# Where 1/z is applied in an attention kernel: as a scale by partition for tiles turned by DMA, as a row for tiles turned on TensorE

## The chip, the core and the metric

The kernel runs on one core of one Trainium2 chip. The core has five engines that each work through their own list of instructions in order and wait for one another by semaphores: TensorE (PE: matmuls; PEld is its loading of weights), VectorE (DVE), ScalarE (ACT), GpSimd (POOL) and SyncE (SP), which here issues all DMAs. The metric is the device time of one execution in microseconds (us).

## The reference

Two stages, the second on the output of the first. `q` is (4, 12288, 128), `kv` is (4, 384, 32, 128).

```python
kv_pool = kv.reshape(B, H // 4, 4, W // 4, 4, C).mean(axis=(2, 4))
k = v = kv_pool.reshape(B, -1, C) @ w_sr          # 768 keys a batch
s = (q @ k.transpose(0, 2, 1)) / sqrt(C)
a = exp(s - s.max(-1)); a /= a.sum(-1) + 1e-9
x = a @ v                                         # the input of the second stage
gate = sigmoid(causal_conv5(x, conv_w))           # 5 taps along the sequence
out = (gate * (x @ w_val)) @ w_out
```

## The kernel before

A batch has 24 groups of 512 queries, so there are 96 groups, and a group has four tiles j = 0 to 3 of 128 queries. All instructions are written by hand in the order in which each engine runs them; one loop goes over the 384 tiles, and each pass of it also carries steps of earlier and later groups: in the pass of tile j of group g stand the scores of the next tile, a part of the av product of group g-2 (`avg`), the conv of group g-3 (`xg`), the second matmuls of group g-4 (`mg`) and the store of a pair of groups.

A tile's path: `score` (L250) puts 128 x 768 scores into a pair of PSUM banks (there are three pairs; a pair is free again when the tile's low pass has read it). `row_max` (L256, DVE) gives the negated maximum by row. `expo` (L268, ACT) replaces the scores by exp and gives the sum z by row, through a second instruction that reads ACT's accumulator. What follows needs the probabilities with keys on partitions, as two fp16 parts (high, and what high leaves over) of 2^15 times the exp. `p_hi` (L315, ACT) and `p_lo` (L319, DVE, one tile later) make the parts. For tiles 0 to 2 (`NX = 3`) they are made with queries on partitions (`hl`) and turned by DMA (`dma_start_transpose`, L323: tiles 0 and 1 in one DMA, tile 2 in another). For tile 3 exp goes to SBUF (`pf`), PE turns it in six matmuls (`turn`, L298), and both passes work on the turned tile (`pt`). `av_part` (L332) then multiplies `pt` by the split values, 18 matmuls a group in four parts.

The division by z comes at the end: the four sums of a group are columns of a tile `z`, ACT adds 1e-9 (`norm_eps`, L272), DVE takes one reciprocal of 128 x 4 (L275), PE turns it (L278), DVE copies the four rows out (L285), a DMA writes them to DRAM (`rd`), and another reads them back as one row of 512 on all 128 partitions (`rb`, L291). `g_x` (L349) multiplies av by the row and by a scale by partition. The matmul outputs `m` of `norm_turn`, of the value matmul (`g_val`, L388) and of the output matmul (`g_out`, L398) share one PSUM bank.

The keys and values of the next batch are made during the current one: `setup_steps` is a list of steps of which the loop takes one at tile 3 of each group, from the second group of a batch on. The first 16 load pieces of kv (the first one loads three pieces, each later one the piece two ahead) and hand back a pooling (`pool_kv`, L121, DVE) that runs at tile 0 of the next group; then come two projections with key splits, and the value splits. Small DVE work (`trickle`) is dripped into the loop two pieces a tile. The weights of the second stage arrive as 64-bit floats and are converted by 14 DVE instructions (`load_moe`, L90 to L97), of which eight run between the poolings of the first batch, ahead of the loop, and the rest from the third tile of the second group on.

After the loop a tail finishes the last four groups, with the last group cut into halves.

Of the kernel before, what the change touches and what calls it, by code (L numbers as in the profile page):

```python
# [16 lines left out]
P = 128  # L17
GQ = 512
NT = GQ // P
NX = 3  # L20
# [7 lines left out]
def attn_moe_kernel(ctx, tc, qT, kvT, w_sr, w_moe, outT):  # L28
# [165 lines left out]
    trickle = []  # L194

# [63 lines left out]
    def on_pe(j):  # L259

        return j >= NX

    def expo(g, j):
        if j == 0:
            g.z = zs[g.i % len(zs)]
        if on_pe(j):
            g.pf[j] = pfp.tile([P, NK], F32, name="pf")
        nc.scalar.activation(out=halves(g.pf[j]) if on_pe(j) else g.s[j], in_=g.s[j],  # L268
                             func=AF.Exp, bias=g.nm.pop(j), accum_out=g.z[:, j:j + 1])

    def norm_eps(g):
        nc.scalar.activation(out=g.z[:, :NT], in_=g.z[:, :NT], func=AF.Copy, bias=1e-9)  # L272

    def norm_reciprocal(g):
        nc.vector.reciprocal(out=g.z[:, :NT], in_=g.z[:, :NT])  # L275

    def norm_turn(g, m):
        nc.tensor.transpose(m[:, :P], g.z, ident)  # L278
        g.rm = m[:NT, :P]

    def norm_store(g):

        r = small.tile([NT, P], F32, name="r")
        g.rd = dram.tile([NT, P], F32, name="rd")
        nc.vector.tensor_copy(out=r, in_=g.rm)  # L285
        nc.sync.dma_start(out=g.rd, in_=r)

    def norm_rows(g):
        g.rb = work.tile([C, GQ], F32, name="rb", bufs=3)
        row = g.rd.rearrange("(o j) p -> o (j p)", o=1)  # L290
        nc.sync.dma_start(out=g.rb, in_=row.broadcast_to([C, GQ]))  # L291
# [14 lines left out]
    def part(g, j, a):  # L306

        if on_pe(j):
            return pt_tile(g)[:, j, a * NCH:(a + 1) * NCH].rearrange("p (h k) q -> p h (k q)", h=2)
        if g.hl is None:  # L310
            g.hl = hlp.tile([P, NX, 2, NK], F16, name="hl")
        return halves(g.hl[:, j, a])

    def p_hi(g, j):
        nc.scalar.activation(out=part(g, j, 0), in_=g.s[j], func=AF.Copy, scale=2.0 ** 15)  # L315

    def p_lo(g, j):

        nc.vector.scalar_tensor_tensor(out=part(g, j, 1), in0=g.s.pop(j), scalar=2.0 ** 15,  # L319
                                       in1=part(g, j, 0), op0=ALU.mult, op1=ALU.subtract)  # L320
        if j in (1, 2):
            j0 = 0 if j == 1 else j
# [25 lines left out]
    def g_x(g, av, c0=0, c1=GQ):  # L348
        nc.vector.scalar_tensor_tensor(out=g.x[:, HALO + c0:HALO + c1], in0=av,  # L349
                                       scalar=g.st["down"], in1=g.rb[:, c0:c1],  # L350
                                       op0=ALU.mult, op1=ALU.mult)
# [89 lines left out]
    for i in range(PIECES):  # L441
# [5 lines left out]
        if i >= 8 and convert:  # L447
            convert.pop(0)()
# [21 lines left out]
    for t in range(NT * G):  # L470
# [7 lines left out]
        if t == NT + 2:  # L478
# [16 lines left out]
        if on_pe(j):  # L495
# [70 lines left out]
    avs = [bank()[:, :half] for _ in cuts]
    av_range(n1, avs[0], 0, len(AV_ORDER), 0, NT // 2)
    h = g_h(n2.th, n2.m)
    av_range(n1, avs[1], 0, len(AV_ORDER), NT // 2, NT)
    n3.m = g_val(n3, misc())  # L570
    n2.m = g_out(h, bank())
    ths = []
    n1.th = work.tile([C, GQ], F32, name="th")
    for av, c in zip(avs, cuts):
        g_x(n1, av, *c)
        ths.append(g_tanh(conv_dve(n1, *c), n1.th[:, c[0]:c[1]]))
# [3 lines left out]
    n3.th = g_tanh(n3.gate)  # L580
    h = g_h(n3.th, n3.m)
    ms = [g_val(n1, bank()[:, :half], *c) for c in cuts]
    hs = [g_h(th, m) for th, m in zip(ths, ms)]
    n3.m = g_out(h, misc())
# [33 lines left out]
```

## Time and profile before

| what | value |
|---|---|
| median of 3 runs | 1134.94 us (1133.9 to 1135.04) |
| profiled execution | 1133.22 us |
| its span (first to last instruction) | 1131.4 us |
| mean granted clock of TensorE | 0.983 |
| DVE row max, L256 | 384, mean 949 ns |
| DMA, queue of SP | 214.48 MB, 85.4% of 16 engines' span |
| transposes by DMA, L323 | 192 |
| rows of 1/z, `rb` | 96 of 256 KB |

A profile row reads: line, engine, operation, output <- input by the program's names, shapes, count, then busy time and mean duration of one, and idle time of the engine just before with what ended it. A row of the timeline begins with its start and duration in us instead; a bracket at its end is the idle time before it and the engine, tile and line that ended it.

### The profile page before, as it was taken

The page shows a single profiled execution, that of the slowest core. Times are in us where ns is not written, and L with a number is a line of the kernel's source. Part 1 is how long each engine was busy: PE and PEld are TensorE (multiplying, and loading weights), DVE is VectorE, ACT ScalarE, POOL GpSimd, SP SyncE. Part 2 cuts the span into 40 slices and gives each one's busy share as a digit, 9 for nine tenths or more (in the row PEclk, how much of TensorE's full clock was granted, in tenths as well). Part 3 has the DMA queues.
Part 4 walks back from the last instruction along what each step waited for, and adds up shares of the span by engine and source line. Part 5 has one row for each costly group of instructions (what it writes and reads, how often), then busy time and mean ns, then how long its engine had stood idle before and what let it go on. Part 6 is the DMA issues. An engine that isn't in the chain of part 4 may idle for free.

```text
span 1131.4 us, 16595 instructions
## 1 busy us (share of the span) xinstructions
PE 1063.6 (94%) x5174; PEld 715.6 (63%) x5174; DVE 919.0 (81%) x1290; ACT 910.4 (80%) x1659; POOL 864.4 (76%) x948
## 2 busy tenths in 40 slices
PE   2879999999979999999997999999999999999996
PEld 1656666666756666666764666666666666666663
DVE  6868888888858888888885888888888888888884
ACT  1868888888858888888885888888888888888881
POOL 1168788878858888888885888887888888888872
PEclk9989999999989999999998999999999999999998
DMA  7779999887879999888876999898788888888872
GB/s 271 145 178 200 211 210 232 192 178 191 187 169 198 202 224 214 206 177 191 187 165 170 209 217 226 200 221 183 171 171 197 187 170 202 186 170 199 175 148 93
DMA packets 487095, 215.53 MB, mean 190 GB/s; under 512 B 453088, under 2 KB 453856, under 8 KB 487008
## 3 DMA queue, kind: packets, MB, share of 16 engines
q1 hardware_dynamic: 487008, 214.48, 85.4%
q8 instruction: 41, 0.67, 0.2%
q14 instruction: 46, 0.38, 0.1%
HBM read 75.83 MB, written 25.36 MB: 89 GB/s over the span
## 4 chain that ended last, share of the span: by engine, by line
PE 49%; DVE 25%; ACT 11%; issue 6%; POOL 5%; DMA 3%; SPq 1%; DVEq 0%; ACTq 0%
PE s L250 17%; PE av L332 16%; PE m L388 8%; DVE nm L256 8%; POOL ql L236 5%; ACT s L268 5%; DVE pool L121 4%; DVE pt L319 4%; ACT hl L315 4%; DVE x L349 4%; PE m L398 3%; PE s L298 3%; DMA kvt<-in_kv 3%; ACT qh L232 2%; DVE h L393 2%
## 5 line engine op out<-in xcount | busy, mean ns | idle before, releaser
L368 POOL TENSOR_TENSOR sum<-sum,tap 128x512 f32<-128x512 f32 x282 | 359.6, 1275 | 39.7 <-ACT tap L357 17.8
L332 PE MATMUL av<-pt,vh 128*128 128x512 f16 x1140 | 389.1, 383 | 0.0
L256 DVE TENSOR_REDUCE nm<-s 128x1 f32<-128x768 f32 x384 | 364.4, 949 | 3.7 <-PE s L250 3.7
L268 ACT ACTIVATE s<-s,nm 128x768 f32<-128x768 f32 x288 | 251.9, 875 | 125.5 <-DVE nm L256 124.3
L359 POOL TENSOR_SCALAR tap<-x,wm 128x512 f32<-128x512 f32 x376 | 253.4, 693 | 82.4 <-DVE x L349 80.9
L319 DVE SCALAR_TENSOR_TENSOR hl<-s,hl 128x768 f16<-128x768 f32 x288 | 273.1, 948 | 21.0 <-ACT hl L315 20.3
L250 PE MATMUL s<-kh,qh 128*128 128x384 f32 x768 | 253.3, 411 | 10.8 <-DVE hl L319 8.1
L315 ACT ACTIVATE hl<-s 128x768 f16<-128x768 f32 x288 | 233.3, 810 | 9.1
L332 PEld LDWEIGHTS <-vh 128*128 128x128 f16 x1164 | 114.0, 98 | 175.5 <-issue 85.8
L332 PE MATMUL av<-pt,vl 128*128 128x512 f16 x570 | 217.5, 382 | 0.0
L236 POOL TENSOR_TENSOR ql<-q,qh 128x512 fp32r<-128x512 f32 x96 | 121.8, 1269 | 122.6 <-ACT qh L232 122.6
L250 PE MATMUL s<-kh,ql 128*128 128x384 f32 x768 | 199.1, 341 | 0.0
L250 PE MATMUL s<-kl,qh 128*128 128x384 f32 x768 | 198.9, 340 | 0.0
L250 PEld LDWEIGHTS s<-kh,qh 128*128 128x128 f32 x768 | 132.4, 193 | 51.8 <-DVE hl L319 8.4
L349 DVE SCALAR_TENSOR_TENSOR x<-av,down,rb 128x512 f32<-128x512 f32 x95 | 71.4, 751 | 89.6 <-POOL ql L236 71.5
L250 PEld LDWEIGHTS s<-kl,qh 128*128 128x128 f32 x768 | 141.3, 190 | 0.5 <-DVE kl L147 0.5
L250 PEld LDWEIGHTS s<-kh,ql 128*128 128x128 f32 x768 | 140.9, 190 | 0.0
L388 PE MATMUL m<-x,wm 128*128 128x512 f32 x188 | 103.0, 630 | 25.0 <-DVE r L285 24.9
L368 POOL TENSOR_TENSOR sum<-tap,tap 128x512 f32<-128x512 f32 x94 | 120.4, 1281 | 0.0
L393 DVE SCALAR_TENSOR_TENSOR h<-th,m 128x512 f32<-128x512 f32 x94 | 64.7, 689 | 59.2 <-PE m L388 57.7
L315 ACT ACTIVATE pt<-s 128x768 f16<-128x768 f32 x96 | 77.8, 810 | 37.8 <-PE s L298 37.8
L332 PEld LDWEIGHTS <-vl 128*128 128x128 f16 x582 | 57.6, 99 | 77.9 <-issue 55.2
(68 smaller groups left out, 1068.9 us busy)
## 6 DMA issues: line engine op xcount, KB each, us to landing
kvt<-in_kv SPq DMA_DIRECT2D x64, 384.0 KB
rb<-rd SPq DMA_DIRECT2D x96, 256.0 KB
q<-in_q SPq DMA_DIRECT2D x47, 512.0 KB
out<-o SPq DMA_DIRECT2D x46, 512.0 KB
pt<-hl SPq DMA_TRANSPOSE x192
rd<-r SPq DMA_DIRECT2D x96, 2.0 KB
out<-o SPq DMA_DIRECT2D x3, 256.0 KB
q<-in_q SPq DMA_DIRECT2D x2, 256.0 KB
```

What stands on the lines that cost most here:

```text
L236: nc.gpsimd.tensor_tensor(out=g.ql, in0=g.q, in1=g.qh.bitcast(F32), op=ALU.subtract)
L250: nc.tensor.matmul(s[:, h, :HALF], a[:, sl], k[:, h * HALF:(h + 1) * HALF], start=(i == 0), stop=(i == 2))
L256: nc.vector.tensor_reduce(out=nm, in_=g.s[j], axis=AX.XY, op=ALU.max, negate=True)
L268: nc.scalar.activation(out=halves(g.pf[j]) if on_pe(j) else g.s[j], in_=g.s[j], func=AF.Exp, bias=g.nm.pop(j), accum_out=g.z[:, j:j + 1])
L315: nc.scalar.activation(out=part(g, j, 0), in_=g.s[j], func=AF.Copy, scale=2.0 ** 15)
L319: nc.vector.scalar_tensor_tensor(out=part(g, j, 1), in0=g.s.pop(j), scalar=2.0 ** 15, in1=part(g, j, 0), op0=ALU.mult, op1=ALU.subtract)
L332: nc.tensor.matmul(out, g.st[v][:, k * P:(k + 1) * P], g.pt[:, j0:j1, a * NCH + k], start=(i == 0), stop=(i == len(AV_ORDER) - 1))
L349: nc.vector.scalar_tensor_tensor(out=g.x[:, HALO + c0:HALO + c1], in0=av, scalar=g.st["down"], in1=g.rb[:, c0:c1], op0=ALU.mult, op1=ALU.mult)
L359: eng.tensor_scalar(out=g.tap[k], in0=src, scalar1=w, scalar2=1.0, op0=ALU.mult, op1=ALU.mult)
L368: nc.gpsimd.tensor_tensor(out=s, in0=acc, in1=g.tap[k], op=ALU.add)
L388: nc.tensor.matmul(m, wval, g.x[:, HALO + c0:HALO + c1], start=True, stop=True)
L393: nc.vector.scalar_tensor_tensor(out=h, in0=th, scalar=1.0, in1=m, op0=ALU.add, op1=ALU.mult)
```

## The change

Every even group of a batch now has all four tiles turned by DMA (`by_dma = 4`), every odd one three as before. For a tile turned by DMA, z stays a column of its own (`zr`): DVE adds 1e-9 and multiplies by 2^-15 in one instruction and takes the reciprocal in a second one, and both passes of that tile use the result as their scale by partition, in place of the constant 2^15. Only the tile turned on PE keeps the way by row, now with one row of 128 instead of four, and only in odd groups. `norm_eps` is gone from ACT. `g_x` becomes a product with the scale by partition alone for the columns of DMA-turned tiles, and keeps the row for the last 128 columns of odd groups.

In the loop, ACT's other work of a tile (tanh, a tap, the cast of q, the evacuation of an output) now stands between exp and the high pass. On DVE the order of a tile is row max, low pass of the tile before, h (tile 1), reciprocal of this tile. Pooling runs at tile 3, two groups after the step that loaded its first pieces (a batch's list has one step more). The conversions all run in the loop, from its fourth tile on. The transposes of an even group go in two pairs. The tail is written in another order.

```diff
-    def on_pe(j):
-        return j >= NX
+    def on_pe(g, j):
+        return j >= g.by_dma
     def expo(g, j):
-        if j == 0:
-            g.z = zs[g.i % len(zs)]
-        if on_pe(j):
+        if on_pe(g, j):
             g.pf[j] = pfp.tile([P, NK], F32, name="pf")
-        nc.scalar.activation(out=halves(g.pf[j]) if on_pe(j) else g.s[j], in_=g.s[j],
-                             func=AF.Exp, bias=g.nm.pop(j), accum_out=g.z[:, j:j + 1])
-    def norm_eps(g):
...
-    def norm_reciprocal(g):
...
+            g.z = zs[g.i // 2 % len(zs)]
+            g.r[j] = g.z[:, :1]
+        else:
+            g.r[j] = small.tile([P, 1], F32, name="zr")
+        nc.scalar.activation(out=halves(g.pf[j]) if on_pe(g, j) else g.s[j], in_=g.s[j],
+                             func=AF.Exp, bias=g.nm.pop(j), accum_out=g.r[j])
+    def reciprocal(g, j):
+        r = g.r[j]
+        nc.vector.tensor_scalar(out=r, in0=r, scalar1=1e-9,
+                                scalar2=1.0 if on_pe(g, j) else 2.0 ** -15,
+                                op0=ALU.add, op1=ALU.mult)
+        nc.vector.reciprocal(out=r, in_=r)
...
+    def p_scale(g, j):
+        return 2.0 ** 15 if on_pe(g, j) else g.r[j]
     def p_hi(g, j):
-        nc.scalar.activation(out=part(g, j, 0), in_=g.s[j], func=AF.Copy, scale=2.0 ** 15)
+        nc.scalar.activation(out=part(g, j, 0), in_=g.s[j], func=AF.Copy, scale=p_scale(g, j))
     def p_lo(g, j):
-        nc.vector.scalar_tensor_tensor(out=part(g, j, 1), in0=g.s.pop(j), scalar=2.0 ** 15,
+        nc.vector.scalar_tensor_tensor(out=part(g, j, 1), in0=g.s.pop(j), scalar=p_scale(g, j),
                                        in1=part(g, j, 0), op0=ALU.mult, op1=ALU.subtract)
-        if j in (1, 2):
-            j0 = 0 if j == 1 else j
+        if (j % 2 or j == g.by_dma - 1) and not on_pe(g, j):
+            j0 = j // 2 * 2
...
     def g_x(g, av, c0=0, c1=GQ):
-        nc.vector.scalar_tensor_tensor(out=g.x[:, HALO + c0:HALO + c1], in0=av,
-                                       scalar=g.st["down"], in1=g.rb[:, c0:c1],
-                                       op0=ALU.mult, op1=ALU.mult)
+        mid = min(c1, g.by_dma * P)
+        if c0 < mid:
+            nc.vector.tensor_scalar_mul(out=g.x[:, HALO + c0:HALO + mid], in0=av[:, :mid - c0],
+                                        scalar1=g.st["down"])
+        if mid < c1:
+            nc.vector.scalar_tensor_tensor(out=g.x[:, HALO + mid:HALO + c1], in0=av[:, mid - c0:],
+                                           scalar=g.st["down"], in1=g.rb[:, mid - c1:],
+                                           op0=ALU.mult, op1=ALU.mult)
...
     def setup_steps(b, st):
         def piece(i):
             if i == 0:
                 key_tiles(st)
+            else:
+                pooling.append(lambda: pool_kv(st, i - 1))
             for k in range(3) if i == 0 else (i + 2,):
                 if k < PIECES:
                     load_kv(b, st, k)
-            return None, lambda: pool_kv(st, i)
-        steps = [lambda i=i: piece(i) for i in range(PIECES)]
+        steps = [lambda i=i: piece(i) for i in range(PIECES + 1)]
...
+            g.by_dma = 4 - i % 2
...
         row_max(cur, j)
         expo(cur, j)
-        if on_pe(j):
+        if on_pe(cur, j):
             turn(cur, j)
-            norm_eps(cur)
-            if mg:
-                out_tile(mg)
-                g_evac(mg, mg.m)
-        p_hi(cur, j)
         if mg and j == 0:
             mg.th = g_tanh(mg.gate)
         if xg and j == 1:
             tap(xg, TAPS - 1, nc.scalar)
-        if last and j == 0:
-            norm_reciprocal(last)
-        if last and j == 1:
+        if at(gi + 2) and j == 2:
+            g_qh(at(gi + 2))
+        if mg and j == 3:
+            out_tile(mg)
+            g_evac(mg, mg.m)
+        turned = last and on_pe(last, NT - 1)
+        if turned and j == 1:
             norm_store(last)
         drip()
         if prev:
             p_lo(prev, (j - 1) % NT)
+        if mg and j == 1:
+            mg.h = g_h(mg.th, mg.m)
+        reciprocal(cur, j)
+        p_hi(cur, j)
         if low and (j == 0 or t < NT):
             low()
             low = None
-        if last and j == 0:
+        if pooling and j == NT - 1:
+            pooling.pop(0)()
+        if turned and j == 0:
             norm_turn(last, misc())
         drip()
-        if mg and j == 1:
-            mg.h = g_h(mg.th, mg.m)
```

In the tail, after the loop, the av product of the second-last group now comes first, the last low pass and the way of its row of 1/z follow, and the two halves of the last group take turns with the output steps of the two groups before it:

```diff
-    norm_reciprocal(n1)
-    p_lo(n1, NT - 1)
-    store_pair(n5)
+    av_part(n2, 0)
     norm_turn(n1, misc())
     n4.th = g_tanh(n4.gate)
-    norm_store(n1)
-    n4.m = g_val(n4, misc())
-    av_part(n2, 0)
-    norm_rows(n1)
     tap(n3, TAPS - 1, nc.scalar)
     g_conv(n3)
-    h = g_h(n4.th, n4.m)
+    p_lo(n1, NT - 1)
+    norm_store(n1)
+    store_pair(n5)
...
```

More of the change, by code (lines that the diff above doesn't have):

```diff
@@ L19 @@
 NT = GQ // P
-NX = 3
 class Group:
@@ L194, in attn_moe_kernel @@
     trickle = []
+    pooling = []
     def value_steps(st):
@@ L257, in row_max @@
         g.nm[j] = nm
-    def on_pe(j):
-        return j >= NX
+    def on_pe(g, j):
+        return j >= g.by_dma
     def expo(g, j):
-        if j == 0:
-            g.z = zs[g.i % len(zs)]
-        if on_pe(j):
+        if on_pe(g, j):
             g.pf[j] = pfp.tile([P, NK], F32, name="pf")
-        nc.scalar.activation(out=halves(g.pf[j]) if on_pe(j) else g.s[j], in_=g.s[j],
-                             func=AF.Exp, bias=g.nm.pop(j), accum_out=g.z[:, j:j + 1])
-    def norm_eps(g):
-        nc.scalar.activation(out=g.z[:, :NT], in_=g.z[:, :NT], func=AF.Copy, bias=1e-9)
-    def norm_reciprocal(g):
-        nc.vector.reciprocal(out=g.z[:, :NT], in_=g.z[:, :NT])
+            g.z = zs[g.i // 2 % len(zs)]
[10 more added lines that the diff above has]
+        nc.vector.reciprocal(out=r, in_=r)
     def norm_turn(g, m):
         nc.tensor.transpose(m[:, :P], g.z, ident)
-        g.rm = m[:NT, :P]
+        g.rm = m[:1, :P]
     def norm_store(g):
-        r = small.tile([NT, P], F32, name="r")
-        g.rd = dram.tile([NT, P], F32, name="rd")
+        r = small.tile([1, P], F32, name="r")
+        g.rd = dram.tile([1, P], F32, name="rd")
         nc.vector.tensor_copy(out=r, in_=g.rm)
@@ L288, in norm_rows @@
     def norm_rows(g):
-        g.rb = work.tile([C, GQ], F32, name="rb", bufs=3)
-        row = g.rd.rearrange("(o j) p -> o (j p)", o=1)
-        nc.sync.dma_start(out=g.rb, in_=row.broadcast_to([C, GQ]))
+        g.rb = work.tile([C, P], F32, name="rb", bufs=3)
+        nc.sync.dma_start(out=g.rb, in_=g.rd.broadcast_to([C, P]))
     def turn(g, j):
@@ L306, in part @@
     def part(g, j, a):
[L308 removed]
+        if on_pe(g, j):
             return pt_tile(g)[:, j, a * NCH:(a + 1) * NCH].rearrange("p (h k) q -> p h (k q)", h=2)
         if g.hl is None:
[L311 removed]
+            g.hl = hlp.tile([P, NT, 2, NK], F16, name="hl")
         return halves(g.hl[:, j, a])
+    def p_scale(g, j):
+        return 2.0 ** 15 if on_pe(g, j) else g.r[j]
     def p_hi(g, j):
[L315 removed]
+        nc.scalar.activation(out=part(g, j, 0), in_=g.s[j], func=AF.Copy, scale=p_scale(g, j))
     def p_lo(g, j):
[L319 removed]
+        nc.vector.scalar_tensor_tensor(out=part(g, j, 1), in0=g.s.pop(j), scalar=p_scale(g, j),
                                        in1=part(g, j, 0), op0=ALU.mult, op1=ALU.subtract)
[L321 to L322 removed]
+        if (j % 2 or j == g.by_dma - 1) and not on_pe(g, j):
+            j0 = j // 2 * 2
             nc.sync.dma_start_transpose(
@@ L525, in attn_moe_kernel @@
             g_conv(xg)
-        if last and j == 3:
+        if turned and j == 3:
             norm_rows(last)
         if at(gi + 2) and j == 2:
-            g_qh(at(gi + 2))
             g_ql(at(gi + 2))
@@ L563, in attn_moe_kernel @@
     store(n4)
+    avs = [bank()[:, :half] for _ in cuts]
+    for i, av in enumerate(avs):
+        av_range(n1, av, 0, len(AV_ORDER), i * NT // 2, (i + 1) * NT // 2)
     n2.th = g_tanh(conv_dve(n2))
     new_x(n1, n2, nc.scalar.copy)
[L566 to L569, printed above, removed]
-    n3.m = g_val(n3, misc())
[L571 to L576, printed above, removed]
+    g_x(n1, avs[0], *cuts[0])
+    h2 = g_h(n2.th, n2.m)
+    n2.m = g_out(h2, bank())
+    n1.th = work.tile([C, GQ], F32, name="th")
+    ths = [g_tanh(conv_dve(n1, *cuts[0]), n1.th[:, :half])]
+    n3.m = g_val(n3, misc())
+    n3.th = g_tanh(n3.gate)
     out_tile(n2)
@@ L579, in attn_moe_kernel @@
     store(n2)
[L580 to L584, printed above, removed]
+    g_x(n1, avs[1], *cuts[1])
+    h3 = g_h(n3.th, n3.m)
+    ms = [g_val(n1, bank()[:, :half], *cuts[0])]
+    n3.m = g_out(h3, misc())
+    ths.append(g_tanh(conv_dve(n1, *cuts[1]), n1.th[:, half:]))
     g_evac(n3, n3.m)
     store(n3)
-    for h, c in zip(hs, cuts):
-        g_evac(n1, g_out(h, bank()[:, :half]), *c)
+    ms.append(g_val(n1, bank()[:, :half], *cuts[1]))
+    for th, m, c in zip(ths, ms, cuts):
+        g_evac(n1, g_out(g_h(th, m), bank()[:, :half]), *c)
         store(n1, *c)
```

12 lines of the change are left out of this document (6 added, 6 removed).

## The prediction

> **What bounds the kernel now.** I read the page first, then stretches of equal work, then one group engine by engine. "Group" is 512 queries (four tiles of 128); there are 96.
>
> ```profile
> span 1131.4 us, 16595 instructions
> PE 1063.6 (94%) x5174; PEld 715.6 (63%) x5174; DVE 919.0 (81%) x1290; ACT 910.4 (80%) x1659; POOL 864.4 (76%) x948
> ```
>
> TensorE (PE) leads, but an average says nothing of a stage. The next view takes stretches from one row max (L256) to another; its columns are length, busy time and count of L256 alone, granted clock, DMA share and GB/s. Four row maxima make a group.
>
> ```profile
> 28.06:56.97 28.91, 11.38 (x13) 0.94 0.75 144
> 56.97:74.23 17.26, 3.79 (x4) 0.80 0.71 167
> 318.23:338.33 20.10, 3.81 (x5) 0.83 0.82 197
> 592.96:614.09 21.13, 3.80 (x4) 0.76 0.79 193
> 338.33:504.63 166.30, 56.93 (x61) 1.00 0.93 204
> 504.63:538.48 33.85, 11.38 (x12) 1.00 0.93 185
> 858.11:1081.19 223.08, 79.71 (x84) 1.00 0.84 182
> ```
>
> There are four kinds of group. Plain ones take 223.08 / 21 = 10.62 us. Those that also pool a piece of the next batch's kv take 166.30 / 15 = 11.09 (a count of 61 holds the row max at the far edge). Those that project or split keys and values take 33.85 / 3 = 11.28. And three, one for each later batch, take 17 to 21 us. From 56.97 to the last group's start (1091.8) I count 45 pooling groups, the three long ones, 15 with projections or splits, and 29 plain: 1034.8 us. The same stretches with all engines (PE busy first):
>
> ```profile
> 338.33:504.63 166.30, 163.26 (x796) 108.58 (x795) 143.38 (x197) 141.58 (x256) 137.44 (x150) 1.00 0.93 204
> 858.11:1081.19 223.08, 223.08 (x1115) 153.19 (x1114) 183.24 (x253) 195.88 (x358) 192.57 (x210) 1.00 0.84 182
> ```
>
> Plain groups are PE without a gap. Pooling groups lose 0.2 us of PE each, and something more in restarts. The waits name the cause of the long groups:
>
> ```profile
> DVE pool L121 <- DMA kvt<-in_kv: 25.2, 8, 7.0
> 601.86 0.95 DVE L121 TENSOR_REDUCE pool<-kvt 128x48 f32<-128x768 f32 x1 [7.03 <-DMA kvt<-in_kv]
> ```
>
> VectorE (DVE) reaches the first pooling just after its load was issued and stands 7 us; everything behind it stands too, and the clock of that stretch falls to 0.76. Against 11.09 the three cost 6.2 + 9.0 + 10.0 = 25.2 us.
>
> One pooling group, first DVE, then ScalarE (ACT), then PE:
>
> ```profile
> 404.87 0.95 DVE L256 TENSOR_REDUCE nm<-s 128x1 f32<-128x768 f32 x1
> ...
> 406.66 0.94 DVE L121 TENSOR_REDUCE pool<-kvt 128x48 f32<-128x768 f32 x1
> 407.52 0.95 DVE L256 TENSOR_REDUCE nm<-s 128x1 f32<-128x768 f32 x1
> 408.39 0.27 DVE L285 COPY r<-m 4x128 f32<-4x128 f32 x1
> ...
> 409.95 0.69 DVE L393 SCALAR_TENSOR_TENSOR h<-th,m 128x512 f32<-128x512 f32 x1 [0.42 <-PE m L388]
> ...
> 415.29 0.75 DVE L349 SCALAR_TENSOR_TENSOR x<-av,down,rb 128x512 f32<-128x512 f32 x1 [0.86 <-POOL ql L236]
> 415.95 0.95 DVE L256 TENSOR_REDUCE nm<-s 128x1 f32<-128x768 f32 x1
> ```
> ```profile
> 405.86 0.88 ACT L268 ACTIVATE s<-s,nm 128x768 f32<-128x768 f32 x1 [0.25 <-DVE nm L256]
> 406.65 0.19 ACT L268 ACTIVATION_READ_ACCUMULATOR s<-s,nm 128x1 f32 x1
> 406.88 0.81 ACT L315 ACTIVATE hl<-s 128x768 f16<-128x768 f32 x1
> 407.58 0.62 ACT L384 ACTIVATE th<-sum 128x512 f32<-128x512 f32 x1
> ...
> 413.33 0.61 ACT L232 CAST qh<-q 128x512 fp32r<-128x512 f32 x1
> 413.84 0.90 ACT L268 ACTIVATE pf<-s,nm 128x768 f32<-128x768 f32 x1
> ```
> ```profile
> 408.71 1.12 PE L388 MATMUL m<-x,wm 128*128 128x512 f32 x2 [0.20 <-DVE r L285]
> ...
> 412.44 0.38 PE L332 MATMUL av<-pt,vh 128*128 128x512 f16 x1
> ...
> 413.71 0.39 PE L332 MATMUL av<-pt,vh 128*128 128x512 f16 x1
> ...
> 415.02 0.82 PE L298 MATMUL s<-ident,pf 128*128 128x128 f32 x6
> ```
>
> Back to back, a DVE instruction starts 0.085 before the printed end of the one ahead (415.29 + 0.75 against 415.95), an ACT one 0.1 before. A hand-off between DVE and ACT takes about 0.04 (row max ends 405.82, exp starts 405.86). An av matmul is 0.218 apart (six from 413.71 to 415.02), so the scores of a tile take 413.71 - 412.44 - 0.22 = 1.05. ACT now goes straight from exp to the high pass (L315); nothing of DVE stands between them.
>
> **The change, part by part.** Prices of the new instructions come from these rows:
>
> ```profile
> L268 ACT ACTIVATE pf<-s,nm 128x768 f32<-128x768 f32 x96 | 86.8, 905 | 0.0
> L319 DVE SCALAR_TENSOR_TENSOR hl<-s,hl 128x768 f16<-128x768 f32 x288 | 273.1, 948 | 21.0 <-ACT hl L315 20.3 <-DVE r L285 0.4
> L393 DVE SCALAR_TENSOR_TENSOR h<-th,m 128x512 f32<-128x512 f32 x94 | 64.7, 689 | 59.2 <-PE m L388 57.7 <-ACT th L384 1.5
> L275 DVE RECIPROCAL z<-z 128x4 f32<-128x4 f32 x96 | 16.1, 168 | 0.0
> L167 DVE TENSOR_SCALAR pw<-pw 128x1 f32<-128x1 f32 x4 | 0.5, 134 | 0.0
> L374 DVE TENSOR_SCALAR fast<-x,wm 128x512 f32<-128x512 f32 x1 | 0.5, 489 | 0.1
> ```
>
> *PE.* Every second group loses six turning matmuls and the turn of z, 0.6 + 0.1 us, which leaves PE 10.62 - 0.35 = 10.27 a group on average. That is a gain only if nothing else is later.
>
> *Scale by partition.* The high pass now reads a scale per partition. Below: no extra, 0.81 (its row above). Above: exp to SBUF, which has a bias per partition, 0.905. I take 0.905. For the low pass, L349 (a per-partition scalar, 0.75) and L393 (none, 0.69) differ by 0.06: 0.95 to 1.01, I take 1.01.
>
> *Reciprocal per tile.* Two small dependent instructions, 0.14 (L167) and about 0.16 (one column of L275's four), in place of one per group. Their issue is small; their place is not. DVE (the row max of the next tile ends each piece):
>
> ```order
> L256 TENSOR_REDUCE nm<-s 128x1
> L285 COPY r<-m 4x128
> L319 SCALAR_TENSOR_TENSOR hl<-s,hl 128x768
> L393 SCALAR_TENSOR_TENSOR h<-th,m 128x512
> L256 TENSOR_REDUCE nm<-s 128x1
> ```
>
> That is tile 1 before. In the changed kernel, an even group:
>
> ```order
> L257 TENSOR_REDUCE nm<-s 128x1
> L290 COPY r<-m 1x128
> L326 SCALAR_TENSOR_TENSOR hl<-s,zr,hl 128x768
> L405 SCALAR_TENSOR_TENSOR h<-th,m 128x512
> L277 TENSOR_SCALAR zr<-zr 128x1
> L280 RECIPROCAL zr<-zr 128x1
> L257 TENSOR_REDUCE nm<-s 128x1
> ```
>
> The reciprocal stands behind the previous tile's low pass (L326) and h (L405), and ACT's high pass waits for it. So there is now a ring: high pass of tile t, low pass of t, reciprocal of t+1, high pass of t+1. The end of tile 3, in the changed kernel (before, the pooling stood in tile 0, behind L319 pt):
>
> ```order
> L326 SCALAR_TENSOR_TENSOR hl<-s,zr,hl 128x768
> L277 TENSOR_SCALAR zr<-zr 128x1
> L280 RECIPROCAL zr<-zr 128x1
> L120 TENSOR_REDUCE pool<-kvt 128x48
> L358 TENSOR_SCALAR x<-av,down 128x512
> L257 TENSOR_REDUCE nm<-s 128x1
> ```
>
> Pooling and x now come between the last reciprocal and the next group's first row max. Tile 1 on ACT, changed kernel: the filler (tap) has moved between exp and high pass.
>
> ```order
> L271 ACTIVATE s,zr<-s,nm 128x2x384
> L369 ACTIVATE tap_1428<-x,wm 128x512
> L322 ACTIVATE hl<-s,zr 128x768
> L271 ACTIVATE s,zr<-s,nm 128x2x384
> ```
>
> *The ring of an even pooling group*, from its first row max at 0. Row max ends 0.95; exp 0.99; sum read 1.78 to 1.97; scale-and-add 2.01, reciprocal 2.19, row max of tile 1 at 2.27, copy 3.14 to 3.41, which frees the bank for the value matmul at 3.45. From there to h took 1.24 (408.71 to 409.95): 4.69. H issues in 0.605: 5.30; reciprocal 5.48 to 5.64; high pass of tile 1 at 5.68; row max of tile 2 from 5.56 to 6.51, so exp 6.55, read 7.34, qh 7.57, high pass of tile 2 at 8.08 (its reciprocal is ready), ending 8.98; exp of tile 3 at 8.88. Low pass of tile 2 at 9.02, its successor 0.925 later, 9.95; reciprocal 10.13; pooling 10.21; x 11.07; next row max **11.73**. An odd group has no copy: th follows the sum read, high pass of tile 0 at 2.54 to 3.45, low pass 3.49, h 4.42 instead of 4.69, so 0.30 less with rounding; its x is two instructions (384 columns 0.62 and 128 columns 0.35, from L349's rate of 0.53 per 512 plus 0.22), 0.14 more. **11.57**; mean 11.65, against 11.09 now.
>
> *Without pooling*, x waits for PE instead: the next scores need the bank that the low pass of tile 1 leaves at 7.63; scores 1.05 and 0.1 for weights that no longer load under cover, then six av matmuls and the hand-off, x at 10.40. Even 11.06, odd 10.90, mean 10.98 against 10.62. The 15 groups with projections have one 128x384 pass more between reciprocal and row max; I take 0.4, so 11.38 (bounds 0 and the 0.66 that they pay today).
>
> *x as a tensor-scalar.* No row reads PSUM in that form: 0.49 (L374, from SBUF) to 0.75 (L349, from PSUM). I take 0.75, the same memory. The Trainium skill (VectorE: DVE Perf Modes, "Why PSUM operands drop a tier") says that a PSUM operand has one read port and leaves fp32 at the single rate; by it 0.75 stands, and if the faster rate held, 0.25 a group, some 23 us in all, would go. No run here shows it.
>
> *Loads ahead of pooling.* A piece is now pooled two groups after its first loads. The 25.2 us go, and nothing else in those groups was later than DVE's wait.
>
> *DMA.* Per two groups seven tiles are turned instead of six, and rows of 1/z shrink from 2 x 256 KB to 64 KB. At 204 GB/s the latter frees 2.2 us; the former costs about 1.3 to 2 (SP spends 2.65 on a pair). The share stays near 0.9 of a longer group; I count nothing.
>
> *Start.* The conversions leave the lead-in (about -1.1, then the last kv piece is late) and go to groups 1 and 2, where the ring also applies: 28.91 becomes about 30.8. Together +0.8, bounds -1 and +3.
>
> *Tail.*
>
> ```profile
> 1110.58 0.75 DVE L349 SCALAR_TENSOR_TENSOR x<-av,down,rb 128x512 f32<-128x512 f32 x1 [4.88 <-PE av L332]
> 1123.75 0.69 DVE L393 SCALAR_TENSOR_TENSOR h<-th,m 128x512 f32<-128x512 f32 x1 [1.48 <-ACT th L384]
> 1126.60 0.42 DVE L393 SCALAR_TENSOR_TENSOR h<-th,s 128x256 f32<-128x256 f32 x1 [1.83 <-PE m L398]
> ```
>
> The new order starts av at once and alternates the halves; of these 8.2 us of waits I take 5.5, bounds 2 and 7.5.
>
> *Sum.* 48 x 11.65 + 29 x 10.98 + 15 x 11.38 = 1048.3 against 1034.8: +13.5, the 25.2 already in it. With +0.8 and -5.5: **+8.8**. The profiled execution took 1133.2, so 1142.0; the median of the runs shown lies 1.7 above it, hence **1143**.
>
> **Rivals.**
> *Cheap ring (faster).* With every new price at its low end (high pass 0.81, low pass 0.95, x 0.49, hand-offs 0.03) the same ring gives 11.15 pooling, 10.43 plain, 10.83 with projections: 1000 us, -35, with start and tail about 1096. It decides from 0.15 us a group less than I count. For: each price is a few hundredths. Against: every low end but x's has a nearer row above it.
> *PE stays the bound (faster).* If DVE's reciprocals never delay ACT, groups run at PE's 10.27 (10.5 with pooling, where DVE's issue alone fills that) and the total is near 1060. It needs the ring under 2.57 a tile; h in tile 1 alone makes it 3.1.
> *Late transposes (slower).* The second pair of an even group is issued in the next group and must land within it. It would decide if a tile took over half more than now; about 1165.
> *Clock.* PE gains gaps of up to 0.6 us. Today gaps of 0.2 leave 1.00, gaps of 7 give 0.76. The Trainium skill (TensorE: Matmul & The Clock Gate, "A second HAM failure mode: psum-queue depth-cycling") tells of short gaps that made the clock oscillate; at half clock in a quarter of the time PE would be the bound again, at about 11.7 a group, from where it adds: 1170.
>
> **How the numbers follow.** Ring as counted 0.55 (own range 1128 to 1160), no difference 0.10 (the ring's loss equals the 25 us and the tail), cheap ring 0.20 and PE bound 0.08, late transposes or clock 0.07. The range reaches into the cheap ring: 1102 to 1163. Faster than 1134.9 by over 0.2% (what a measurement here can tell) 0.30, within 0.10, slower 0.60.
>
> **What would show it.** Right: ACT's high pass waiting for the reciprocal, in tile 1 most; PE with gaps in plain groups; no wait of pooling for kvt; pooling groups near 11.65. Wrong: plain groups still without a gap on PE, an x of 0.5, or high passes that never wait.

## The result, and the profile after

The changed kernel takes 1149.22 us (median of 4 runs, 1147.87 to 1150.32) against 1134.42 for the kernel before on the same chip (4 runs, 1132.55 to 1135.04): 1.0133 times as long, 95% interval 1.0115 to 1.0150. The forecast was 1143.0, so slower came out, by 6 us more than forecast; as a difference it is +14.8 us where +8.1 (1143.0 against 1134.9) was forecast. The profiled execution took 1150.32 us.

The head of its page: VectorE's share goes from 81 to 90%, and TensorE's busy time hardly moves although it has 336 fewer matmuls.

```profile
span 1148.5 us, 16451 instructions
PE 1068.7 (93%) x4838; PEld 662.8 (58%) x4838; DVE 1032.9 (90%) x1962; ACT 908.6 (79%) x1563; POOL 863.1 (75%) x948
```

Stretches between two first row maxima (now L257) of groups; columns are length, busy time of L257 with its count, granted clock, DMA share and GB/s. The start (groups 0 to 2), and one of the groups with projections:

```profile
27.23:61.50 34.27, 11.38 (x12) 0.85 0.64 126
280.02:292.74 12.72, 3.78 (x4) 1.00 0.88 173
```

Then 15 groups with pooling and 15 without, for all engines (PE, PEld, DVE, ACT, POOL, each busy time with its count, then clock, DMA share and GB/s):

```profile
361.35:534.61 173.26, 165.32 (x743) 100.66 (x744) 160.17 (x301) 139.73 (x240) 137.06 (x150) 1.00 0.93 195
926.12:1091.97 165.85, 162.69 (x745) 101.11 (x743) 148.90 (x287) 140.37 (x241) 137.20 (x150) 1.00 0.84 174
```

Groups with pooling take 173.26 / 15 = 11.55 us (before 11.09), plain ones 165.85 / 15 = 11.06 (before 10.62). In groups with pooling VectorE is busy 160.2 of 173.3 us; before it was 143.4 of 166.3. TensorE now has gaps in plain groups too. The waits of the whole execution (total, times, longest):

```profile
ACT hl L322 <- DVE zr L280: 63.1, 96, 1.8
DVE hl L326 <- ACT hl L322: 38.4, 221, 0.4
PEld s L251 <- DVE hl L326: 25.0, 42, 0.6
DVE zr L277 <- ACT s L271: 18.5, 87, 1.1
DVE pool L120 <- DMA kvt<-in_kv: 5.7, 6, 2.7
```

The 7 us waits of pooling for kvt are gone from the loop (19.8 us in three groups before); the 5.7 us that are left lie ahead of the loop, in the poolings of the first batch (5.4 before). In their place stand the pairs that the order of instructions let one expect: the high pass waits for the reciprocal, the low pass for the high pass, the reciprocal for the sum of exp, and the scores for the low pass that frees their bank. Here is VectorE in one odd group with pooling, three tiles of which are turned by DMA (columns: start, duration, then what it is, and the idle time ahead of it):

```profile
407.57 0.95 DVE L257 TENSOR_REDUCE nm<-s 128x1 f32<-128x768 f32 x1
...
409.63 0.15 DVE L277 TENSOR_SCALAR zr<-zr 128x1 f32<-128x1 f32 x1 [0.20 <-ACT s L271]
...
411.00 1.02 DVE L326 SCALAR_TENSOR_TENSOR hl<-s,zr,hl 128x768 f16<-128x768 f32 x1 [0.16 <-ACT hl L322]
...
412.53 0.15 DVE L277 TENSOR_SCALAR zr<-zr 128x1 f32<-128x1 f32 x1
412.71 0.16 DVE L280 RECIPROCAL zr<-zr 128x1 f32<-128x1 f32 x1
412.79 0.94 DVE L257 TENSOR_REDUCE nm<-s 128x1 f32<-128x768 f32 x1
413.90 1.02 DVE L326 SCALAR_TENSOR_TENSOR hl<-s,zr,hl 128x768 f16<-128x768 f32 x1 [0.17 <-ACT hl L322]
...
416.23 1.02 DVE L326 SCALAR_TENSOR_TENSOR hl<-s,zr,hl 128x768 f16<-128x768 f32 x1 [0.17 <-ACT hl L322]
...
419.06 0.94 DVE L257 TENSOR_REDUCE nm<-s 128x1 f32<-128x768 f32 x1
```

From 407.57 to 419.06, 11.49 us, VectorE's named waits are 0.20 + 0.16 + 0.17 + 0.17 = 0.70. A reciprocal pair holds it for 0.26 (412.53 to 412.79), four a group 1.04. Two readings are open: either these waits, passed round between ScalarE and VectorE, set the pace (the ring of the prediction), or VectorE is simply full and the waits are what is left. The prediction's sum holds both; the experiments part them, though not wholly.

The prices, from the groups by form of the page (busy, mean ns):

```profile
L326 DVE SCALAR_TENSOR_TENSOR hl<-s,zr,hl 128x768 f16<-128x768 f32 x336 | 340.9, 1015 | 38.8 <-ACT hl L322 38.4
L358 DVE TENSOR_SCALAR x<-av,down 128x512 f32<-128x512 f32 x48 | 35.8, 746 | 7.1 <-PE av L339 7.1
L322 ACT ACTIVATE hl<-s,zr 128x768 f16<-128x768 f32 x336 | 302.9, 901 | 74.5 <-DVE zr L280 63.1 <-DVE down L170 3.7 <-DVE up L167 2.4
```

### The profile page after: what moved, and what is told of

Its sections match the earlier page's. It is cut to its first block, busy times and chain, and to the rows that moved or that the text cites. A ratio compares the mean times of both kernels' runs of the same rounds, so it can differ in the third digit from the quotient of the medians.

```text
span 1148.5 us, 16451 instructions
## 1 busy us (share of the span) xinstructions
PE 1068.7 (93%) x4838; PEld 662.8 (58%) x4838; DVE 1032.9 (90%) x1962; ACT 908.6 (79%) x1563; POOL 863.1 (75%) x948
## 5 line engine op out<-in xcount | busy, mean ns | idle before, releaser
L326 DVE SCALAR_TENSOR_TENSOR hl<-s,zr,hl 128x768 f16<-128x768 f32 x336 | 340.9, 1015 | 38.8 <-ACT hl L322 38.4
L257 DVE TENSOR_REDUCE nm<-s 128x1 f32<-128x768 f32 x384 | 361.4, 941 | 1.4 <-PE s L251 1.4
L271 ACT ACTIVATE s<-s,nm 128x768 f32<-128x768 f32 x336 | 293.9, 875 | 86.4 <-DVE nm L257 85.8
L322 ACT ACTIVATE hl<-s,zr 128x768 f16<-128x768 f32 x336 | 302.9, 901 | 74.5 <-DVE zr L280 63.1
L251 PE MATMUL s<-kh,qh 128*128 128x384 f32 x768 | 239.2, 392 | 30.9 <-DVE zr L277 13.4
L251 PEld LDWEIGHTS s<-kh,qh 128*128 128x128 f32 x768 | 121.8, 191 | 145.0 <-issue 72.9
L400 PE MATMUL m<-x,wm 128*128 128x512 f32 x188 | 99.8, 612 | 6.1 <-DVE r L290 6.0
L410 PE MATMUL m<-h,wm 128*128 128x512 f32 x188 | 96.0, 592 | 1.7 <-DVE h L405 1.7
L358 DVE TENSOR_SCALAR x<-av,down 128x512 f32<-128x512 f32 x95 | 64.6, 680 | 13.3 <-PE av L339 13.3
```

The lines of the kernel that those rows point to most:

```text
L251: nc.tensor.matmul(s[:, h, :HALF], a[:, sl], k[:, h * HALF:(h + 1) * HALF], start=(i == 0), stop=(i == 2))
L257: nc.vector.tensor_reduce(out=nm, in_=g.s[j], axis=AX.XY, op=ALU.max, negate=True)
L271: nc.scalar.activation(out=halves(g.pf[j]) if on_pe(g, j) else g.s[j], in_=g.s[j], func=AF.Exp, bias=g.nm.pop(j), accum_out=g.r[j])
L358: nc.vector.tensor_scalar_mul(out=g.x[:, HALO + c0:HALO + mid], in0=av[:, :mid - c0], scalar1=g.st["down"])
L400: nc.tensor.matmul(m, wval, g.x[:, HALO + c0:HALO + c1], start=True, stop=True)
L410: nc.tensor.matmul(m, wout, h, start=True, stop=True)
```

## The experiments

Theories. *Ring*: the high pass waits for a reciprocal that stands behind the low pass of the tile before, and this wait sets the period. *VectorE's load*: the new instructions fill VectorE, and the waits only show that. *Price*: a scale by partition makes the passes longer. *Turning*: the other split between DMA and TensorE helps or hurts by itself. A difference of two kernels' groups is read from the same kinds of stretches as above, 8 to 18 groups each. The runs stand on several chips, on which the kernel before takes 1132.5 to 1134.6 us (medians), so a difference of two runs is good to about 2 us; four runs each stand behind the kernels with a ratio, one behind the others.

**Kv alone, and kv with the tail.** The kernel before with the pooling one group later:

```diff
+    pooling = []
...
+            else:
+                pooling.append(lambda: pool_kv(st, i - 1))
-            return None, lambda: pool_kv(st, i)
-        steps = [lambda i=i: piece(i) for i in range(PIECES)]
+        steps = [lambda i=i: piece(i) for i in range(PIECES + 1)]
...
+        if pooling and j == 0:
+            pooling.pop(0)()
```

> The kernel before with one part of the change alone: each piece of the next batch's kv is pooled one group later, still in tile 0, behind the low pass. All theories: the 7 us waits of pooling for kvt go, and pooling groups stay at 11.1 us, plain ones at 10.62. If the 25.2 us of the prediction are wholly gone and nothing else was late in those groups: about 1109 us (ratio 0.978). Rival: another transfer or engine is late behind the kv wait, then less than half of it is gained, 1122 or more.

1105.5 us, ratio 0.9761 (0.9746 to 0.9775). Nothing else was late in the three long groups; the 25.2 us that they took over 11.09 came back, and 15 groups with pooling took 166.32 / 15 = 11.09:

```profile
343.45:509.77 166.32, 163.32 (x796) 108.70 (x795) 143.37 (x197) 141.61 (x256) 137.44 (x150) 1.00 0.94 206
```

The second kernel takes the changed kernel's tail as well (with the one reciprocal of the last group ahead of it).

> As the run with kv alone, and the order of the tail as in the changed kernel. If the tail's gain of about 5 us does not depend on where 1/z is applied: about 1104 us. If the earlier matmuls of the last groups merely wait for rows of 1/z (which here all four tiles still need): about 1109 us, no gain.

1102.34 us, ratio 0.9732 (0.9718 to 0.9747): 3.2 us below the run with kv alone. So two parts of the change give 30 us on their chip (1132.46 to 1102.34). The changed kernel stands 14.8 above the kernel before, so the rest takes about 45: 1/z by partition, the other turning, the new order on ScalarE and VectorE and the conversions in the loop.

**Turning alone.** On top of the last kernel:

```diff
-    def on_pe(j):
-        return j >= NX
+    def on_pe(g, j):
+        return j >= 4 - g.i % 2
...
-        if j in (1, 2):
-            j0 = 0 if j == 1 else j
+        if not on_pe(g, j) and (j % 2 or on_pe(g, j + 1)):
+            j0 = j // 2 * 2
...
```

> As the run with kv and tail, and every second group all DMA-turned, with rows of 1/z for all tiles as in the kernel before: the turning part of the change without the scale by partition. If TensorE bounds the groups and DMA can carry it: 0.3 us a group less, plain groups near 10.3, about 25 us below the run with kv and tail, near 1080 us. Rival, DMA: at a share of 0.93 in pooling groups the seventh turned tile of each two groups makes transposes late; no gain or a loss, 1104 to 1140 us.

1102.12 us, ratio 0.9728 (0.9712 to 0.9744): no gain. Eight groups with pooling and 16 without:

```profile
412.25:500.93 88.68, 85.29 (x402) 55.48 (x400) 76.46 (x105) 75.07 (x137) 73.27 (x80) 1.00 1.04 232
886.84:1053.96 167.12, 166.42 (x802) 111.68 (x801) 139.92 (x193) 148.36 (x273) 146.71 (x160) 1.00 1.01 205
```

Plain groups took 167.12 / 16 = 10.45 with TensorE busy for 166.42 of the 167.12, so the turning gave 0.17 a group against 10.62, about half of the 0.3 that was expected. Those with pooling stayed at 88.68 / 8 = 11.09, with TensorE busy for 85.29 / 8 = 10.66 of it, so these groups had never been TensorE's. Outside this window six groups with pooling took 11.4 to 13.0, and TensorE waited 6.5 us in all for transposes, about what the 29 plain groups gained (29 x 0.17 = 4.9). One of the eight, VectorE and TensorE:

```profile
414.04 0.94 DVE L121 TENSOR_REDUCE pool<-kvt 128x48 f32<-128x768 f32 x1
414.90 0.95 DVE L258 TENSOR_REDUCE nm<-s 128x1 f32<-128x768 f32 x1
415.76 0.27 DVE L287 COPY r<-m 4x128 f32<-4x128 f32 x1
...
422.65 0.75 DVE L351 SCALAR_TENSOR_TENSOR x<-av,down,rb 128x512 f32<-128x512 f32 x1 [0.86 <-POOL ql L238]
```
```profile
416.09 1.12 PE L390 MATMUL m<-x,wm 128*128 128x512 f32 x2 [0.53 <-DVE r L287]
```

Pooling in tile 0 delays the next row max, which delays the copy that frees the bank of the value matmul, and TensorE stands 0.53 us. Further on in the same group VectorE has 0.86 idle us ahead of x.

**Pooling moved to that gap.** The kernel with kv and tail, pooling in tile 3 ahead of x, where the changed kernel has it (`j == 0` becomes `j == 3`).

> The kernel with kv and tail (1102.3 us), but with pooling at the end of tile 3, ahead of x, where the changed kernel has it. In the kernel before VectorE stands idle 0.86 us there, waiting for the last av matmul, and pooling issues in 0.85. If pooling groups owe their 0.47 us to pooling's place in tile 0 (it delays the next row max, the copy that frees the bank, and so the value matmul): 45 groups at 10.62 to 10.7, about 1082 us. If DMA or VectorE's load as such bounds pooling groups: still 11.09, 1102 us. If x becomes late: over 11.09, slower.

1079.77 us, ratio 0.9526 (0.9512 to 0.9540). Groups with and without pooling now cost the same, 159.20 / 15 = 10.61, and TensorE has no gap in either:

```profile
335.55:494.75 159.20, 159.20 (x796) 109.38 (x795) 143.67 (x196) 140.02 (x256) 137.91 (x150) 1.00 1.02 218
862.62:1022.02 159.40, 159.40 (x797) 109.39 (x796) 130.90 (x181) 140.02 (x256) 137.84 (x150) 1.00 0.86 186
```

This speaks for place, not load: VectorE is as busy as before (143.7 us), and the DMA share of 1.02 costs nothing here.

**With the turning as well.**

> As the run just above, with every second group all DMA-turned and rows of 1/z for all tiles. With pooling out of tile 0, the fewer TensorE instructions count in pooling groups as well: about 10.45 a group as in the plain ones (10.61 and 10.28 in turn), 13 us below the run above, near 1070 us. Rival, DMA: pooling groups would have to move 1.06 times the bytes per time at a share of 0.93; transposes come late in some groups (four groups of over 11.4 were seen in the run of turning alone), no gain.

1098.26 us, ratio 0.9685 (0.9669 to 0.9701): 18 us worse than without the turning. The DMA rival holds. From the waits and the windows:

```profile
PE av L334 <- DMA pt<-hl: 23.4, 16, 3.0
```
```profile
342.58:509.57 166.99, 158.67 (x750) 104.98 (x749) 144.57 (x196) 138.68 (x256) 137.61 (x150) 0.99 1.05 228
```

At 228 GB/s the transposes come up to 3.0 us late, and 15 groups with pooling take 11.13 on average where TensorE is busy for 10.58: odd groups 10.29, even ones 10.6 to 14.6. The rate alone does not tell when they are late: the eight groups of the run of turning alone moved 232 GB/s, and each took 11.07 to 11.10.

**The turning in the last batch only**, where no kv is loaded:

```diff
-        return j >= 4 - g.i % 2
+        return j >= (4 - g.i % 2 if g.b == B - 1 else NT - 1)
```

> As the run with kv, tail and pooling in tile 3 (1079.8 us), with every second group all DMA-turned in the last batch alone, where no kv is loaded; rows of 1/z for all tiles as before the change. If transposes were late in the run with turning everywhere only beside loads of kv: no group of the last batch over 10.65 but those with splits, some ten of them at 10.28 instead of 10.61, about 1076.5 us (ratio 0.950). If the transposes are late anyhow: 1080 us or more.

1075.50 us, ratio 0.9485 (0.9466 to 0.9504), the fastest of all. 18 groups of the last batch took 10.44 on average, and no transpose was late:

```profile
840.51:1028.51 188.00, 187.22 (x902) 125.59 (x901) 157.40 (x218) 167.02 (x307) 165.39 (x180) 1.00 1.02 205
```

**The changed kernel without the wait for the reciprocal.**

```diff
+    fixed = const.tile([P, 1], F32, name="fixed")
+    nc.vector.memset(fixed, 2.0 ** 15)
...
-        return 2.0 ** 15 if on_pe(g, j) else g.r[j]
+        return 2.0 ** 15 if on_pe(g, j) else fixed
```

> The changed kernel, but the high and low passes of DMA-turned tiles take their scale from a constant column (2^15) instead of 1/z: the division is left out for them, while every instruction and the scale by partition stay and the high pass no longer waits for the reciprocal. Ring theory: the waits of ACT for the reciprocal (0.5 to 0.8 us in tile 1 of each group) leave the path; about 0.4 us a group, groups of 11.15 (pooling) and 10.6 (plain), near 1112 us. Rival, VectorE's own load (its new instructions fill it, the wait only shows that): pooling groups stay within 0.05 of 11.55, plain ones lose about 0.2, near 1142 us. Rival, price of the scale by partition alone: no change, 1149.

1133.97 us in one run: 15 below the changed kernel, between the two theories. The two kinds of groups differ:

```profile
356.82:529.02 172.20, 165.29 (x744) 100.58 (x745) 159.98 (x301) 138.16 (x241) 136.85 (x150) 1.00 0.96 198
915.19:1087.04 171.85, 171.84 (x794) 107.19 (x793) 158.40 (x306) 147.24 (x257) 146.03 (x160) 1.00 0.87 178
```

Plain groups go to 171.85 / 16 = 10.74, 0.32 less; the wait was worth that there. Groups with pooling go to 11.48, 0.07 less: there the ring falls as the cause. VectorE in an odd one now has one wait by name, the sum of exp, 0.19 us twice in 11.39 (425.74 to 437.13); in an even one there is 0.28 for the value matmul as well:

```profile
427.81 0.16 DVE L279 TENSOR_SCALAR zr<-zr 128x1 f32<-128x1 f32 x1 [0.19 <-ACT s L273]
...
432.96 0.15 DVE L279 TENSOR_SCALAR zr<-zr 128x1 f32<-128x1 f32 x1 [0.19 <-ACT s L273]
```

**Without the price of the scale.** The constant as an immediate (`return 2.0 ** 15`); 1/z is left out for tiles turned by DMA, as in the run above.

> The changed kernel with the constant 2^15 as the scale of every high and low pass, an immediate as before; the reciprocals are still worked out, and the division is left out for DMA-turned tiles. Beside the fixed column (1134 us, groups of 11.49 with pooling and 10.74 without) this takes away only the price of a scale by partition: 0.09 us of each high pass and 0.06 of each low pass, 3.5 of each a group. VectorE's load theory: the 0.2 us of low passes come off pooling groups nearly whole (11.3 to 11.35), plain ones lose 0.1 to 0.2, near 1122 us. Ring theory: high passes of ScalarE stand on the path too, 0.5 a group, pooling groups near 11.0, near 1095 us. Price of no weight: 1134.

1128.76 us in one run: 5 below the run above, less than either theory had.

```profile
357.34:528.41 171.07, 163.36 (x745) 100.45 (x746) 157.69 (x301) 134.65 (x241) 137.10 (x150) 1.00 0.95 198
912.24:1082.01 169.77, 169.53 (x794) 107.00 (x793) 155.34 (x306) 143.41 (x257) 146.29 (x160) 1.00 0.88 180
```

171.07 / 15 = 11.40 and 169.77 / 16 = 10.61: 0.08 and 0.13 a group for a scale by partition in seven passes of each kind in two groups. Price is the smallest of the three. The average with pooling hides two kinds: odd groups went from 11.39 to 11.25, even ones stayed (11.58 and 11.59). There VectorE waited for what its passes saved, for the sum of exp above all. The first line is the 15 groups with pooling of the run with the fixed column, the second the same groups of this run:

```profile
DVE zr L279 <- ACT s L273: 5.8, 30, 0.2
DVE zr L277 <- ACT s L271: 7.2, 30, 0.3
```

So VectorE is not simply full in these groups. The two small instructions stand ahead of the next row max and must wait for ScalarE's sum of this tile, which reads as a second, smaller ring that neither theory held; no run took that wait away alone.

**Without the two small instructions.** `reciprocal` is left empty, so 1/z is left out and the passes scale by the row sum itself.

> The changed kernel without its two small instructions a tile (add and scale, reciprocal): high and low passes scale by the row sum itself, so 1/z is left out of all tiles. Passes keep their scale by partition. VectorE's load theory: 1.08 us of VectorE's time a group (4 times 0.27 from one row to the next) come off beside the wait for the reciprocal: pooling groups near 11.1, plain ones near 10.5, about 1106 us. Ring theory: the wait alone counts, so as with the fixed column: 11.49 and 10.74, 1134 us.

1084.00 us in one run: 50 below the fixed column, 65 below the changed kernel.

```profile
340.32:502.01 161.69, 159.06 (x743) 101.56 (x743) 143.76 (x181) 135.61 (x240) 137.21 (x150) 1.00 1.01 210
869.60:1038.28 168.68, 167.51 (x794) 109.22 (x793) 141.84 (x178) 145.02 (x257) 146.28 (x160) 1.00 0.87 181
```

161.69 / 15 = 10.78 and 168.68 / 16 = 10.54. Beside the fixed column groups with pooling lose 0.70 of the 1.04 that the pairs hold VectorE for, plain ones 0.20. 384 pairs of instructions on 128 numbers each, with the waits that they bring, are the largest cost of this change. VectorE's load named the right instructions and undersized them (11.1 and 1106 us forecast). With the pairs goes VectorE's wait for the sum of exp too (5.8 / 15 = 0.39 a group above); how much of the 0.70 is the one and how much the other was not separated. What this run keeps (the scale by partition, the turning, the order on ScalarE, the conversions in the loop) can cost little: 1084.00 is 4 us above the kernel with rows of 1/z and pooling in tile 3.

**Three tiles by DMA in every group, 1/z by partition kept** (`g.by_dma = 3`, and one buffer of `z` for each group in turn).

> The changed kernel with three tiles of every group DMA-turned, the fourth PE-turned, as before the change; 1/z by partition stays. The prediction's ring: every group now has the copy of 1/z ahead of the value matmul and an x in two instructions, 11.87 for groups with pooling instead of 11.65 on average, 0.22 a group: 1149 + 20, near 1168 us. VectorE's load theory gives the same instructions and about the same, 1165. Rival, TensorE still sets the pace: 0.35 a group, near 1181. Rival, DMA-turned tiles were what became late: 1149 or less.

1167.02 us in one run, as forecast by ring and load (both hold the same instructions of VectorE: a copy in every group, and x always in two). 176.16 / 15 = 11.74 and 190.30 / 17 = 11.19:

```profile
354.27:530.43 176.16, 170.85 (x800) 107.60 (x798) 162.67 (x316) 139.71 (x241) 136.77 (x150) 1.00 0.84 185
917.34:1107.64 190.30, 188.55 (x903) 121.73 (x902) 171.45 (x342) 157.69 (x273) 155.17 (x170) 1.00 0.76 159
```

So once 1/z goes by partition, the other turning saves 18 us; in the order of before it saved nothing.

**Pooling in tile 2 of the changed kernel** (`j == NT - 1` becomes `j == 2`).

> The changed kernel with pooling at the end of tile 2 instead of tile 3. If pooling groups are slow for pooling's place (as in the kernel before, where tile 0 cost 0.47 us and tile 3 nothing): some tenths of a microsecond a group, 1130 to 1140 us. If VectorE is full wherever it stands: 11.45 to 11.55 against 11.555, 1145 to 1149 us.

1149.44 us in one run, no change. From tile 0 to tile 3 pooling's place was worth 0.48 us a group in the order of before; from tile 3 to tile 2 it is worth 0.02 here (173.01 / 15 = 11.53). Tile 0 was not tried in the changed kernel. Its VectorE has no gap as long as a pooling in the groups shown.

```profile
360.99:534.00 173.01, 165.01 (x745) 99.89 (x743) 160.60 (x302) 141.10 (x241) 136.96 (x150) 1.00 0.93 196
```

**Conversions of the weights back in the lead-in.**

```diff
         pool_kv(st, i)
+        if i >= 8 and convert:
+            convert.pop(0)()
...
-        if t == 3:
+        if t == NT + 2:
             trickle += convert
```

> The changed kernel with the 14 conversion steps of the weights where they were: from kv piece 8 of the lead-in on, the rest from tile 6. If the steps between row max and low pass are what stretched groups 0 to 2 from 28.9 to 34.3 us: they take about 30, the first row max comes 0.8 later at 28.0, and group 3 starts near 58 instead of 61.5: about 1145.5 us. If the reciprocals or the clock in the start did it: group 3 stays at 61.5 or later, 1149 us.

1149.82 us in one run, and group 3 starts at 61.32 instead of 61.50: the conversions are not what stretched the start. Groups 0 to 2 still take 33.38 (34.27 changed, 28.91 before), and the first row max comes 0.71 later.

```profile
27.94:61.32 33.38, 26.87 (x114) 22.16 (x114) 29.61 (x63) 24.12 (x41) 3.89 (x4) 0.85 0.69 129
```

Without the reciprocals the same three groups took 30.43:

```profile
27.22:57.65 30.43, 24.62 (x115) 19.30 (x114) 28.77 (x48) 24.40 (x41) 3.89 (x4) 0.94 0.75 141
```

So 3.84 of the 5.36 us that the start lost are the small instructions and their waits again, and the granted clock goes with them (0.85 with, 0.94 without, 0.94 before). Whether the lower clock lengthens the start or only shows TensorE's gaps was not separated.

## Why the prediction was right, point by point

*Pooling and plain groups.* Forecast 11.65 and 10.98, measured 11.55 and 11.06. The working followed the order on VectorE and ScalarE step by step, and with it got the sign.

*What sets the period.* Here the reading was half right. The prediction called it a ring closed by the high pass waiting for the reciprocal. That wait is there, longest where it was expected (0.49 and 0.81 us in tile 1 of two neighbouring groups):

```profile
412.97 0.90 ACT L322 ACTIVATE hl<-s,zr 128x768 f16<-128x768 f32 x1 [0.49 <-DVE zr L280]
...
424.71 0.90 ACT L322 ACTIVATE hl<-s,zr 128x768 f16<-128x768 f32 x1 [0.81 <-DVE zr L280]
```

Taking it away gave 0.32 us in plain groups but only 0.07 in groups with pooling. There the path runs along VectorE's own queue, with its waits for the sum of exp. The number came out near because the ring's legs counted that queue's instructions and that wait too: for these groups the right time came with the wrong wait.

*Reciprocals.* "Their issue is small; their place is not" is the sentence that failed. Their place was worth 0.07 and 0.32 us a group; they and the waits that they bring were worth 0.77 and 0.52 (11.55 to 10.78, 11.06 to 10.54), 65 us in all.

*Scale by partition.* 0.905 and 1.01 forecast, 0.901 and 1.015 measured; together worth 5 us.

*x as a tensor-scalar.* 0.75 forecast, 0.746 measured, against 0.49 from SBUF. The rule of the Trainium skill (VectorE: DVE Perf Modes, "Why PSUM operands drop a tier") agrees with this row.

*Groups with projections.* Mis-sized. From group 3's start (61.50) to the last group's (1114.05) it is 1052.55 us, forecast 1048.3. By the row maxima of the timeline the 15 groups with projections took 175.8 of it, 11.7 each instead of 11.38. The longest kind, 12.72 in the window above, holds the largest value of each row (0.94 us on VectorE) and the scale of a column (1.32, the last section). The first group with pooling of each batch took 11.98, 12.57 and 12.07 (the rivals below say why).

*Loads ahead of pooling.* Right: 27 us in the run alone. That the list of waits has the same 25.2 as the three long groups is chance: 5.4 of the list's lie ahead of the loop and stayed, and the long groups lost 19.8 to the wait itself and 5.4 to what stood behind it.

*Start.* +0.8 forecast; measured 0.83 earlier and 5.36 longer, +4.5. The step that failed gave the extra time to the conversions and to a ring as in later groups; the conversions are 0.9 of it, the reciprocals with their waits 3.8.

*Tail.* -5.5 forecast. The last group's first row max stands at 1114.05:

```profile
1114.05 0.95 DVE L257 TENSOR_REDUCE nm<-s 128x1 f32<-128x768 f32 x1
```

From there to the end it is 34.5 us against 39.6: -5.1. On the kernel with kv alone the same order gave 3.2.

*Sum.* -0.8 + 5.4 + 17.7 - 5.1 = +17.2 between the two profiled executions (+17.1), against +8.8 forecast: 3.7 of the difference is the start, 4.2 the groups. That the groups came so near is luck in part: groups with pooling were forecast 4.5 us too long in all, plain ones 1.9 too short, those with projections 5.1, the three first ones with pooling 1.7. (The forecast's last step, 1142.0 + 1.7, is 1143.7 and was written as 1143.)

*Rivals.* The cheap ring needed prices at their low ends, and none was. TensorE as the bound at 10.27 is refuted, and the bound itself was put too low: with the turning in the last batch alone groups took 10.44 with TensorE busy for 187.22 of 188.00 us, a gain of 0.17 a group where six turning matmuls in every second group were counted at 0.30. Late transposes: no wait for pt stands by name among the changed kernel's waits, yet they came late three times, in the first group with pooling of each batch. TensorE and the DMA queue at the second one:

```profile
350.61 0.38 PE L339 MATMUL av<-pt,vh 128*128 128x512 f16 x1 [1.03 <-DVE pt L326]
340.18 12.73 SPq L330 DMA_TRANSPOSE pt<-hl  x3
```

The wait is put down to a low pass of the next group, which this product does not read. TensorE's queue waits there for two DMAs, and the trace has the last landing of the transpose issued at 340.18, right behind three loads of kv, at 350.52. Together the three groups took 2.0 us more than others with pooling. In the run of turning with pooling in tile 3 transposes were late in many groups, at 228 GB/s; the changed kernel moves 195, with an eighth of the bytes in rows of 1/z. Whether those bytes or the slower pace spare it was not separated. The clock: 0.85 in the start, but 1.00 in both long stretches although TensorE has gaps there, so the oscillating clock of that rival does not show in them.

*What the prediction took from before.* It read groups with pooling as nearly TensorE's, with 0.2 us of gap. In truth 0.48 of their 11.09 us came from where pooling stood.

## What to carry to other kernels

A pair of 0.26 us on a [128, 1] column is cheap once and dear 384 times on the engine that is about to be the bound, the more so where it must wait for another engine: count an engine's queue by issue time, a group at a time, ahead of looking for waits. A gap in a busy engine's queue names a place to move work to: here 0.86 us of idle VectorE at the end of tile 3 hid a pooling of 0.85 whole, and that one line was worth some 23 us. To tell a wait from a full queue, take away the wait alone and keep every instruction. A wait that is put down to an instruction whose output is not read may be a DMA's.

## What the runs showed of the hardware

The tile of a column's scale (`diag`, 128 x 128 in SBUF times a column) takes 0.28 to 0.39 us in the kernel before and 0.73 to 1.32 in the changed one, the same instruction four times in each. VectorE and GpSimd at one place each, before and changed:

```profile
808.54 2.62 POOL L368 TENSOR_TENSOR sum<-sum,tap 128x512 f32<-128x512 f32 x2
809.51 0.39 DVE L170 TENSOR_SCALAR diag<-ident,up 128x128 f32<-128x128 f32 x1
```
```profile
284.31 3.97 POOL L380 TENSOR_TENSOR sum<-sum,tap 128x512 f32<-128x512 f32 x3
287.04 1.32 DVE L169 TENSOR_SCALAR diag<-ident,up 128x128 f32<-128x128 f32 x1
```

A sum of GpSimd takes about 1.31 us. Before, `diag` starts 0.34 ahead of the first sum's end (808.54 + 1.31 = 809.85) and ends 0.05 behind it; changed, it starts 0.08 behind the second sum's end (286.96 by thirds of 3.97) and ends 0.08 behind the third's (288.28). Both end where GpSimd's running instruction ends, whatever they started at. The Trainium skill (SBUF — State Buffer, "Who interferes with whom") describes an exclusive lock on a port that VectorE and GpSimd share; these two places agree with it, though no run was made for it. By these two places, how long this instruction of VectorE takes is a matter of what GpSimd had begun.
